# A decode step of cached attention with a gated branch: PE's program cut from three instruction blocks to two by a six-turn loop, h and q ahead of the transposes, nine wo rows and the gate ahead of the last V, PE fillers

## Chip, cores, metric

One core of one Trainium2 chip. The metric is device microseconds of one execution, from repeated runs; the spans in the traces are 1.5 to 2.8 us shorter than the times of the same executions. Profiles are of one execution. PE is TensorE (matmuls), DVE is VectorE, ACT is ScalarE, POOL is GpSimd, and SP is SyncE, which issues the loads. A *filler* is a matmul whose result nobody uses, there to keep PE's clock up; PE is called warm at its full granted clock and cold at half of it. In what follows a "row of wo" is one of the 32 slices of 128x448 into which the output projection is cut; each is one contraction of 128.

## The reference, cut

```python
x = A_x                                   # (2, 1, 448) bf16
xn = _layernorm(x)
# attention over the last W = 2048 of 8192 cached positions, 16 query heads, 8 kv heads, Dh = 256
q = (xn @ wq).reshape(B, 1, 16, 256).transpose(0, 2, 1, 3)
k = repeat(k_cache[:, :, Sk - W:, :], 2, axis=1)
v = repeat(v_cache[:, :, Sk - W:, :], 2, axis=1)
p = softmax(einsum("bhqd,bhkd->bhqk", q, k) * Dh ** -0.5)
s = einsum("bhqk,bhkd->bhqd", p, v) @ wo   # after putting the heads back in a row
g = silu(relu(xn @ w1) @ w2)               # Dff = 1792
return x + s * g
```

44.1 MB are read: K and V 16.8 MB each, wq and wo 3.7 MB each, w1 and w2 1.6 MB each. There are four *turns* (2 batches by 2 halves of the kv heads), each with 4.2 MB of K and 4.2 MB of V.

## The kernel before

A small layer records operations for each engine with their dependencies and then emits waits. PE's turns are one loop; what belongs to only some turns is under a branch. In a turn DVE transposes four blocks of K (the scores need the head dimension on the partitions), PE makes scores from each, and after the softmax the P·V product of the turn *before* is scaled and folded into `at_z`, the left side of the wo product.

```python
def turn(u):
    for blk in range(NBLK):
        if u: do_T(u, blk)                         # DVE transposes
        if u > 1 and blk in (1, 2): ...            # attention fold of turn u-2, between them
        do_S(u, blk)                               # PE scores
    if u: do_PV(u - 1)
    softmax(u)
    if u: attend_scale(u - 1)
    if u == 1: do_H(); do_F()                      # the gated branch; F over four column tiles
    if u < NU - 1: turn_q(u + 1)
# [cut]
for blk in range(NBLK): do_T(0, blk)
do_q(); turn_q(0)
# ... turns 0 to 3, with loads between them; the last V has a buffer of its own (wq's):
#     deps = [None if u == 0 else st["q_mm"] if u == NU - 1 else st["PV", u - 1]]
turn(3)
idle_loop(5, 2)                                    # ten filler matmuls
do_PV(3, (0, 1)); attend_turn(2); do_PV(3, (2,)); attend_spread(2); do_PV(3, (3,))
attend_scale(3)
m_f = fold_tiles(g_ap, True, True, [v_f, v_sel])   # gate, on 8 partitions x 112
# [cut: exp] 
attend_turn(3); attend_spread(3)
m_t = do_wo(0, TILED)                              # nine rows over four column tiles
# [cut: fold of these, add, reciprocal, product of the gate]
m_o = do_wo(TILED, 2 * NWO)                        # 23 rows x 4 matmuls of 112 columns
```

Loads go out from one queue in this order: part of wq, K0, the rest of wq, K1, V0, w1, w2, K2, V1, K3, V2, V3, wo in seven parts. At the start PE jumps to a block near the end of its program and back, so that the last block of instructions is fetched then ("the visit").

Of the kernel before, what the change touches and what calls it, by code (L numbers as in the profile page):

```python
# [14 lines left out]
class _Op:  # L15
    __slots__ = ("eng", "fn", "deps", "dma", "needed", "value", "sem", "turn", "group", "token", "gives")

    def __init__(self, eng, fn, deps, dma):
        self.eng, self.fn, self.deps, self.dma = eng, fn, deps, dma
        self.needed, self.value, self.sem = dma, 0, None  # L20
        self.turn, self.group, self.token, self.gives = None, None, None, False


class _Prog:
# [4 lines left out]
    def __init__(self, nc, es):  # L29
        self.nc, self.es = nc, es  # L30
        self.lists = {PE: [], DVE: [], ACTE: [], SP: [], POOL: []}
        self.turn, self.group, self.runs = None, None, {}

    def op(self, eng, fn, deps=(), token=None):
        o = _Op(eng, fn, [d for d in deps if d is not None], False)
        if eng == PE:
            o.turn, o.group, o.token = self.turn, self.group, token
        self.lists[eng].append(o)
        return o
# [6 lines left out]
    def run(self, turns):  # L46
# [6 lines left out]
        taken = {DVE: [], SP: []}  # L53
        for o in pe:
            if o.token is not None:
                assert not o.token.gives
                o.token.gives = True
                taken[o.token.eng].append(o.token)
        for e in taken:
            assert taken[e] == [o for o in self.lists[e] if o.gives]  # L60
# [16 lines left out]
        for e, ops in self.lists.items():  # L77
            sem, count = self.es.enter_context(nc.semaphore(f"s_{e}")), 0
            for o in ops:
                if o.gives:  # L80
                    assert o.dma or not o.needed
                    o.sem = give[e]
# [3 lines left out]
                elif o.needed:  # L86
                    count += 1
                    o.sem, o.value = sem, count
# [22 lines left out]
        for eng, name in ((nc.vector, "dve"), (nc.tensor, "pe")):  # L111
            again[name] = eng.alloc_register(f"{name}_again")
            nc.br("dve_all" if name == "dve" else "pe_visit", engines=[eng.engine])
# [15 lines left out]
        body = [o for o in loop if o.turn == turns - 1]  # L129
        body += [o for o in loop if o.group == "ffn"]  # L130
        with nc.body("pe_all", parent=main, valid_engines=[t.engine]):
            top = nc.cur_bb
# [3 lines left out]
            with t.Fori(0, turns) as i:  # L136
                k = 0
                while k < len(body):
                    g = body[k].group
                    end = next((m for m in range(k, len(body)) if body[m].group != g), len(body))  # L140
                    part, runs = body[k:end], self.runs[g]
                    k = end
                    if runs == list(range(turns)):
                        emit(t, part, seen)
                    elif len(runs) == 1:
                        with t.If(i == runs[0]):
                            emit(t, part, seen)
                    else:
                        assert runs == list(range(runs[0], turns))
                        with t.If(i > runs[0] - 1):  # L150
                            emit(t, part, seen)
            nc.br("pe_past", engines=[t.engine])
            nc.switch_bb("pe_visit", parent=main)
            t.nop()
            nc.br("pe_all", engines=[t.engine])
            nc.switch_bb("pe_past", parent=top)
# [5 lines left out]
def bass_recurrent_scan__sliding_block_cached__dense_activation_relu__decode_kernel(  # L162
# [21 lines left out]
    NU = 4  # L184
# [9 lines left out]
    FIRST = 2  # L194
    NCOL = D // 4
    NROW = 4 * B
    GAP = NROW + 3
    es = contextlib.ExitStack()
    with es:
# [31 lines left out]
        q_n = named("q_n", [128, 512], BF)  # L231
        qz = named("qz", [128, 4 * 64], BF)
        h_n = named("h_n", [128, FC // 4], BF)
        h_t = named("h_t", [128, FC // 4], BF)
        h_z = named("h_z", [128, 14 * GAP], BF)
        x_c = named("x_c", [NROW, NCOL], BF)
        ea = named("ea", [NROW, NCOL], F32)
        g_sb = named("g_sb", [NROW, NCOL], F32)
        tmp = named("tmp", [NROW, NCOL], F32)
# [8 lines left out]
        q_t = named("q_t", [128, 512], F32)  # L248
        ssum = named("ssum", [128, 1], F32)
# [15 lines left out]
        obk_last = psum("obk_last", [128, 512], F32)  # L265
# [13 lines left out]
        d_xc = pr.dma(ACTE, x_c[:, :], A_x[:, 0, :].rearrange("b (i n) -> (b i) n", i=4))  # L279

# [13 lines left out]
        def load_v(u, cuts=(0, NT)):  # L294
            deps = [None if u == 0 else st["q_mm"] if u == NU - 1 else st["PV", u - 1]]
            d_v[u] = []
            for lo, hi in zip(cuts, cuts[1:]):
                d_v[u].append((hi, pr.dma(SP, vbuf[u // (NU - 1)][:, lo * DH:hi * DH],
                                          kv_src(u, A_v_cache)[:, :, lo * DH:hi * DH], deps)))

        d_wq = [pr.dma(SP, wq_sb[:, 0:FIRST * HC], wq_src[:, 0:FIRST * HC])]
        load_k(0)
        d_wq.append(pr.dma(SP, wq_sb[:, FIRST * HC:SLOTS * HC], wq_src[:, FIRST * HC:SLOTS * HC]))
        load_k(1)
        load_v(0)
        st["w1"] = pr.dma(SP, w1_sb[:, 0:W2_AT], w1_src)
        st["w2"] = pr.dma(SP, w2_sb[:, W2_AT:W2_AT + 14 * D].rearrange("p (hf f) -> p hf f", hf=2), w2_src)
# [5 lines left out]
        p_z = [pr.op(POOL, lambda e, t=t: e.memset(t[:, :], 0.0)) for t in (qrep, spread, sel, h_z, at_z)][-1]  # L313

        a_z = [pr.op(ACTE, lambda e, t=t: e.memzero(t[:, :])) for t in (obk, sbk, hbk, fbk, obk_last)][-1]
# [7 lines left out]
        pr.op(ACTE, lambda e: e.activation(tmp[0:B, 0:1], st2[0:B, 0:1], ACT.Exp), [a_sd])  # L323
        for e2 in range(2):
# [39 lines left out]
        for s in range(SLOTS):  # L364
            m_xr = pr.op(PE, mm(mbk_ap(2 * s, 2), xg[0:B, 128 * s + 128:128 * s + 256], ident[0:B, 0:B], s == 0),
                         [v_xn, p_id])
# [56 lines left out]
        def out_bank(u):  # L423
            return obk if u < NU - 1 else obk_last

        def do_PV(u, gs=range(4)):
            bank, src = out_bank(u), vbuf[u // (NU - 1)]
            for g in gs:
                deps, token = [], None
                if u == NU - 1:  # L430
                    deps = [next(d for hi, d in d_v[u] if hi >= 16 * g + 16), st["pt", u]]
                elif g == 0:
                    token = d_v[u][0][1]
                for a in range(2):
                    for i in range(4):
                        t = 16 * g + 4 * i + 2 * a
                        o = pr.op(PE, mm(bank[32 * i:32 * i + 16, :],
                                         pt[:, 8 * t:8 * t + 16], src[:, t * DH:(t + 2) * DH],
                                         g == 0 and a == 0, g == 3 and a == 1, tile_position=(0, 32 * i)), deps, token=token)
                        deps, token = [], None  # L440
            st["PV", u] = o

        def attend_scale(u):
            st["osb", u] = pr.op(DVE, lambda e: e.tensor_scalar(  # L444
                out=o_sb[:, :], in0=view(out_bank(u), 0, [[1, 512]]), scalar1=rs[:, u:u + 1], scalar2=None, op0=ALU.mult),
                [st["PV", u], st["rs", u], st.get(("oT", u - 1))])

        def attend_turn(u):
            deps = [st["osb", u]] if u > 1 else []
            for dhi in range(2):  # L450
                for tp in range(2):
                    o = pr.op(PE, mm(mbk_ap(136 + 8 * dhi, 8), o_sb[:, 256 * tp + 128 * dhi:256 * tp + 128 * dhi + 128],
                                     fold[:, 8 * tp:8 * tp + 8], tp == 0, tp == 1), deps)
                    deps = []
# [6 lines left out]
        def attend_spread(u):  # L461
# [3 lines left out]
                                      [at] if u > 1 else [], token=None if u > 1 else at)  # L465
# [3 lines left out]
        def do_q():  # L469
            deps = d_wq + [v_xr, a_z]  # L470
# [6 lines left out]
            st["q_mm"] = o  # L477
# [5 lines left out]
        def do_H():  # L483
            deps = [st["w1"]]
            for s in range(SLOTS):
                for i in range(4):
                    lo = s * FC + i * (FC // 4)
                    o = pr.op(PE, mm(hbk[32 * i:32 * i + 4, 0:FC // 4], xr[:, 4 * s:4 * s + 4], w1_sb[:, lo:lo + FC // 4],
                                     s == 0, s == SLOTS - 1, tile_position=(0, 32 * i)), deps)
                    deps = []  # L490
            v = pr.op(DVE, lambda e: e.tensor_scalar(
                out=h_n[:, :], in0=hbk[:, 0:FC // 4], scalar1=0.0, scalar2=None, op0=ALU.max), [o])
            v = pr.op(DVE, lambda e: e.transpose(h_t[:, :], view(h_n, 0, [[1, 7], [7, 32]])), [v])
            st["h"] = pr.op(DVE, lambda e: e.tensor_copy(  # L494
                view(h_z, 3, [[GAP, 7], [7 * GAP, 2], [4, 2]]), view(h_t, 0, [[32, 7], [2, 2], [1, 2]])), [v, p_z])
# [13 lines left out]
        def do_F():  # L509
            deps = [st["w2"], st["h"]]  # L510
            for f in range(14):
                st["F"] = tiled(fbk, h_z, f, w2_sb, W2_AT + f * D, 4, 10, deps)
                deps = []

        def idle_work(n, deps=()):
            for _ in range(n):
                pr.op(PE, mm(wbk[:, :], ident[:, :], q_n[:, :], True, True), deps)
                deps = ()

        def idle_loop(n, m):  # L520
            def fn(e):
                with e.Fori(0, n):
                    for _ in range(m):
                        o = mm(wbk[:, :], ident[:, :], q_n[:, :], True, True)(e)
                return o
            pr.op(PE, fn)

        def turn(u):
            pr.turn, pr.group = u, "all"
            for blk in range(NBLK):  # L530
                if u:
                    do_T(u, blk)
                if u > 1 and blk in (1, 2):
                    pr.group = "turn" if blk == 1 else "spread"
                    (attend_turn if blk == 1 else attend_spread)(u - 2)
                    pr.group = "all"
# [109 lines left out]
```

## Time and profile before

| | before |
|---|---|
| time, median | 113.06 us (4 runs; 113.56 when the prediction was made, of 3) |
| span of the profile | 109.8 us |
| DMA queue busy | 95.0% of the span |
| PE, DVE busy | 55%, 57% |
| last row of wo landed | 107.4 us |
| end of the last wo matmul | 108.0 us |

How to read the profile's lines: in a line of the timeline the first two numbers are the start and the length in us; then engine, source line, operation, what it writes and reads, and in square brackets how long the engine idled before it and for whom. In a line of the windows the columns are the stretch, its length, busy time of PE, PEld (weight loads), DVE, ACT and POOL with their counts, granted PE clock, DMA share and GB/s. The lines of before are in the prediction.

Each load lands on 16 DMA engines, and the records of the trace tell when each of the 16 was done. Worked out from them for the kernel before, first and last engine in us: K0 14.97 to 16.59, K1 30.80 to 32.42, K2 57.86 to 59.49, last part of wo 105.86 to 107.39. The last engine is 1.5 us or more behind the first in every load. Up to K2 it is alone (in K0 the other 15 are done by 15.33).

### The profile page before, as it was taken

The numbers are of one execution on the slowest core, as the hardware profiler recorded it, in microseconds if no ns is written. First come the engines' busy times: TensorE is split into PE (matmuls) and PEld (weight loads), VectorE is DVE, ScalarE is ACT, GpSimd is POOL, SyncE is SP. The second block draws the span as 40 slices with busy tenths as digits, with TensorE's granted clock in tenths as the row PEclk, the third lists the DMA queues.
The fourth block names the chain that finished last, engine by engine and source line by source line (L and its number), as shares of the span: only waits on it lengthen the run. The fifth ranks groups of instructions, "written<-read, shape, count | busy, mean of one in ns | idle before, by whom it ended". The sixth has DMA issues, their size and how long they took to land. (4 is left out here: it accounts for less than half of the span.)

```text
span 109.8 us, 1368 instructions
## 1 busy us (share of the span) xinstructions
PE 60.4 (55%) x558; PEld 19.5 (18%) x558; DVE 63.0 (57%) x96; ACT 10.2 (9%) x19; POOL 3.1 (3%) x11
## 2 busy tenths in 40 slices
PE   0001000076599330899755597853039785898993
PEld 0000000020111020000241010112001011534792
DVE  0249109995400459993468999266299926624601
ACT  4990000000000110000200000020000002000000
POOL 7400000000000000000000000000000000000000
PEclk9999999999999995579996569997555899999999
DMA  3998989998899889998899999999999999899950
GB/s 60 502 388 382 549 371 395 439 537 382 382 453 501 382 367 416 411 548 382 382 501 394 406 406 465 441 406 406 465 441 406 444 430 430 361 419 410 402 207 7
DMA packets 3046, 44.15 MB, mean 402 GB/s; under 512 B 354, under 2 KB 612, under 8 KB 1508
## 3 DMA queue, kind: packets, MB, share of 16 engines
q1 hardware_dynamic: 3008, 44.11, 95.0%
q8 instruction: 2, 0.03, 0.1%
q10 hardware_dynamic: 36, 0.01, 0.1%
HBM read 44.11 MB, written 0.00 MB: 402 GB/s over the span
## 5 line engine op out<-in xcount | busy, mean ns | idle before, releaser
L379 DVE STREAM_TRANSPOSE kt<-kbuf 128x2048 f32<-128x2048 f32 x16 | 35.9, 2286 | 7.8 <-DMA kbuf<-in_A_k_cache_dram 7.8
L361 PE MATMUL sbk<-kt,qz 128*8 128x512 bf16 x128 | 31.1, 1073 | 13.6 <-PEq L102 13.5
L401 DVE TENSOR_REDUCE rm<-sbk 128x1 f32<-128x512 f32 x4 | 2.8, 692 | 14.6 <-PE sbk L361 14.6
L361 PE MATMUL obk<-vbuf,xr 128*4 128x512 bf16 x28 | 3.2, 626 | 13.9 <-DMA vbuf<-in_A_wq_dram 13.9
L407 ACT ACTIVATE et<-sbk,bias 128x512 bf16<-128x512 f32 x4 | 2.7, 687 | 81.1 <-DVE bias L405 81.1
L361 PEld LDWEIGHTS sbk<-kt,qz 128*8 128x8 bf16 x128 | 2.6, 87 | 28.9 <-issue 28.7
L361 PE MATMUL pbk<-et,spread 128*128 128x32 bf16 x64 | 2.6, 193 | 7.2 <-PEq L102 7.2
L361 PE MATMUL obk<-vbuf,pt 128*16 128x512 bf16 x96 | 5.8, 381 | 0.0
L361 PE MATMUL mbk<-ident,xg 2*128 2x2 bf16 x7 | 0.3, 163 | 8.5 <-DVE xg L325 8.5
L361 PE MATMUL wbk<-q_n,ident 128*128 128x512 bf16 x15 | 4.1, 395 | 1.4 <-DVE qz L396 1.4
L361 PE MATMUL hbk<-kbuf,at_z 128*8 128x112 bf16 x92 | 4.8, 213 | 0.0
L409 DVE STREAM_TRANSPOSE et<-et 128x512 bf16<-128x512 bf16 x4 | 2.8, 712 | 3.4 <-ACT et L407 3.4
L417 DVE TENSOR_TENSOR pt<-pbk,hmask 128x512 bf16<-128x512 f32 x4 | 2.8, 692 | 3.3 <-PE pbk L361 3.3
L361 PEld LDWEIGHTS hbk<-kbuf,at_z 128*8 128x8 bf16 x92 | 4.6, 87 | 0.1
L361 PEld LDWEIGHTS pbk<-et,spread 128*128 128x128 bf16 x64 | 2.2, 99 | 10.5 <-issue 10.5
L361 PEld LDWEIGHTS obk<-vbuf,pt 128*16 128x16 bf16 x96 | 2.5, 94 | 6.8 <-issue 4.7
L361 PEld LDWEIGHTS obk<-vbuf,xr 128*4 128x4 bf16 x28 | 0.8, 114 | 15.4 <-issue 15.4
L611 DVE TENSOR_TENSOR tmp<-hbk,g_sb 8x112 f32<-8x112 f32 x1 | 0.3, 262 | 4.4 <-PE hbk L361 4.4
L361 PE MATMUL fbk<-wf,h_z 128*2 128x448 bf16 x14 | 1.7, 567 | 1.7 <-DVE h_z L494 1.7
L456 DVE TENSOR_TENSOR at_exp<-mbk,qmask 128x128 bf16<-128x128 f32 x4 | 1.2, 292 | 2.5 <-PE mbk L361 2.5
L361 PE MATMUL obk_last<-vbuf,pt 128*16 128x512 bf16 x32 | 2.3, 380 | 0.0
L444 DVE TENSOR_SCALAR o_sb<-obk,rs 128x512 bf16<-128x512 f32 x3 | 2.2, 731 | 0.0
(80 smaller groups left out, 43.9 us busy)
## 6 DMA issues: line engine op xcount, KB each, us to landing
kbuf<-in_A_k_cache_dram SPq DMA_DIRECT2D x4, 4096.0 KB, 23.4
vbuf<-in_A_v_cache_dram SPq DMA_DIRECT2D x3, 4096.0 KB, 15.8
wf<-in_B_w_dram SPq DMA_DIRECT2D x2, 1568.0 KB, 42.4
vbuf<-in_A_v_cache_dram SPq DMA_DIRECT2D x1, 3072.0 KB, 22.5
vbuf<-in_A_wq_dram SPq DMA_DIRECT2D x1, 2560.0 KB, 20.9
vbuf<-in_A_wq_dram SPq DMA_DIRECT2D x1, 1024.0 KB, 6.1
vbuf<-in_A_v_cache_dram SPq DMA_DIRECT2D x1, 1024.0 KB, 24.4
kbuf<-in_A_wo_dram SPq DMA_DIRECT2D x1, 1008.0 KB, 26.2
```

The lines of the kernel that those rows point to most:

```text
L361: return lambda e: e.matmul(out_ap, lhsT=lhsT, rhs=rhs, start=start, stop=stop, skip_group_check=True, **kw)
L379: st["kt", u, blk] = pr.op(DVE, lambda e: e.transpose(view(dst, 0, [[1, 32 * NT]]), view(src, 32 * blk, [[DH // 2, NT], [1, 32]])), [d_k[u ...
L401: v = pr.op(DVE, lambda e: e.tensor_reduce(out=rm[:, :], in_=sbk[:, :], axis=AX.X, op=ALU.max), [st["S", u, NBLK - 1]])
L407: a = st["exp", u] = pr.op(ACTE, lambda e: e.activation(e_sb, sbk[:, :], ACT.Exp, bias=bias[:, 0:1], accum_out=ssum[:, 0:1]), [v, st.get(( ...
L409: token = pr.op(DVE, lambda e: e.transpose(e_t, e_sb), [a, st.get(("Pt", u - 1))])
L417: st["pt", u] = pr.op(DVE, lambda e: e.tensor_tensor(out=view(pt, 0, [[8, NT], [2, 4], [1, 2]]), in0=view(pbk, 0, [[2, NT], [0, 4], [1, 2] ...
L444: st["osb", u] = pr.op(DVE, lambda e: e.tensor_scalar(out=o_sb[:, :], in0=view(out_bank(u), 0, [[1, 512]]), scalar1=rs[:, u:u + 1], scalar ...
L456: st["at", u] = pr.op(DVE, lambda e: e.tensor_tensor(out=view(at_exp, 0, [[16, 8], [8, 2], [1, 8]]), in0=view(mbk, 136, [[1, 8], [8, 2], [ ...
L611: v_t = pr.op(DVE, lambda e: e.tensor_tensor(out=tmp[:, :], in0=hbk[0:NROW, 0:NCOL], in1=g_sb[:, :], op=ALU.mult), [m_o, v_g])
```

## The change

Its intent: PE's program in two 16 KB blocks instead of three, so that no visit is needed. For that the last P·V moves into the loop (six turns instead of four, groups of operations switched by branches), V3 shares the buffer of V0 to V2, h is made by a loop with register addresses, and wo takes two wide matmuls a row instead of four narrow ones. h and q are ready before the first transposes; the gate and nine wo rows are done while V3 is on its way, with sixteen fillers to keep PE's clock up. The core of the diff, cut:

```diff
-        for blk in range(NBLK):
-            do_T(0, blk)
         do_q()
         turn_q(0)
-        idle_work(1, [st["q"]])
+        m_h = do_H()
+        for blk in range(NBLK):
+            do_T(0, blk)
+            if blk == 1:
+                relu(m_h)
+        pr.op(PE, None, [st["q"]])
@@ turn
+            if u > 1:
+                pr.group = "turn"
+                attend_turn(u - 2)
+                attend_spread(u - 2)
+            if u == NU:
+                pr.group = "ffn"
+                do_F()
+                early_wo()
+                idle_loop(FILL, 2)
@@ loads
-            deps = [None if u == 0 else st["q_mm"] if u == NU - 1 else st["PV", u - 1]]
+            deps = [st["PV", u - 1] if u else None]
         load_v(2)
-        load_v(3, (0, 48, 64))
+        load_w2()
+        turn(3)
         for n in WO_PARTS:
             d_wo[j0] = pr.dma(SP, wo_sb[...], wo_src[...], [st["S", 2, NBLK - 1]])
+            if j0 == 0:
+                load_v(3)
@@ do_F: F untiled, gate on 2 partitions x 448
-                st["F"] = tiled(fbk, h_z, f, w2_sb, W2_AT + f * D, 4, 10, deps)
+                st["F"] = pr.op(PE, mm(view(fbk, 0, [[1, D]], n=B), ..., f == 0, f == 13), deps)
+            v_rc = pr.op(DVE, lambda e: e.reciprocal(tmp[0:B, :], ea[0:B, :]), [v_d])
@@ early_wo
+            deps = [pr.op(DVE, lambda e: e.tensor_copy(sums[:, :], view(tbk, 0, [[1, D]])), [m_t]), v_sel]
+            for t in range(2):
+                pr.op(PE, mm(view(hbk, 0, [[1, NCOL]], n=B, p0=32 * t), view(sel, 3, [[4, 2]]), sums[...],
+                             True, tile_position=(0, 32 * t)), deps)
@@ run
-            nc.br("dve_all" if name == "dve" else "pe_visit", engines=[eng.engine])
+            nc.br(f"{name}_all", engines=[eng.engine])
```

## The prediction

> **What bounds the kernel now.** I read the page's head first, then the DMA queues, the chain of waits, the timeline of the first 35 us and of the last 15 us, and the windows around the end.
>
> The page: engine busy shares, the busy tenths in 40 slices, the DMA queues.
>
> ```profile
> PE 60.4 (55%) x558; PEld 19.5 (18%) x558; DVE 63.0 (57%) x96; ACT 10.2 (9%) x19; POOL 3.1 (3%) x11
> DMA  3998989998899889998899999999999999899950
> q1 hardware_dynamic: 3008, 44.11, 95.0%
> q8 instruction: 2, 0.03, 0.1%
> ```
>
> No compute engine is above 57%, while the one DMA queue is busy 95% of the span and only its first and its last slices are thin. 44.11 MB have to come in; the kernel before is a stream of loads. Two instruction fetches lie in the span, about 16 KB each (0.03 MB by 2).
>
> Windows of equal kind around the end of the stream (PE, PEld, DVE, ACT, POOL busy, clock, DMA share, GB/s):
>
> ```profile
> 105.00:105.50 0.50, 0.50 (x14) 0.50 (x12) 0.00 (x0) 0.00 (x0) 0.00 (x0) 1.00 0.97 357
> 105.50:107.50 2.00, 2.00 (x43) 1.89 (x41) 0.00 (x0) 0.00 (x0) 0.00 (x0) 1.00 0.18 67
> 107.50:109.80 2.30, 0.49 (x8) 0.32 (x8) 0.52 (x2) 0.00 (x0) 0.00 (x0) 1.00 0.03 8
> ```
>
> Most of the 16 DMA engines are done by 105.5, a straggler runs to about 107. PE loads weights almost without a gap until 107.3, then starts its last eight matmuls, which end at 108.0. So the chain of waits, which ends in PE's `hbk` work, is level with the last landing: the stream and the tail end together.
>
> The timeline of the tail (start, us, engine, line, operation):
>
> ```profile
> 90.57 0.69 DVE L401 TENSOR_REDUCE rm<-sbk 128x1 f32<-128x512 f32 x1 [2.17 <-PE sbk L361]
> 94.52 2.32 PE L361 MATMUL wbk<-q_n,ident 128*128 128x512 bf16 x10
> 94.98 0.73 DVE L444 TENSOR_SCALAR o_sb<-obk,rs 128x512 bf16<-128x512 f32 x1
> 96.77 1.04 PE L361 MATMUL obk_last<-vbuf,pt 128*16 128x512 bf16 x16
> 99.24 0.75 DVE L444 TENSOR_SCALAR o_sb<-obk_last,rs 128x512 bf16<-128x512 f32 x1 [0.32 <-PE obk_last L361]
> 100.95 0.23 DVE L466 CAST at_z<-mbk 128x16 bf16<-128x16 f32 x1 [0.28 <-PE mbk L361]
> 102.53 0.84 DVE L607 RECIPROCAL tmp<-ea 8x112 f32<-8x112 f32 x1
> 103.20 4.79 PE L361 MATMUL hbk<-kbuf,at_z 128*8 128x112 bf16 x92
> 108.03 0.26 DVE L611 TENSOR_TENSOR tmp<-hbk,g_sb 8x112 f32<-8x112 f32 x1 [4.37 <-PE hbk L361]
> ```
>
> The reader is to see the distance from the last max (`rm`, 90.57) to the end, 19.3 us, and that the reciprocal of 8x112 takes 0.84 us where the add on the same tile took 0.20.
>
> **What the Trainium skill says.** "TensorE: Matmul & The Clock Gate", Part 1: the array runs at half rate after about 3.4 us of idleness and is warm again after about as long a busy window, 426.7 or 215.7 ns for 512 columns. The trace agrees: ten fillers in 2.32 us are 232 ns each, and q's 28 matmuls after a long idle time, four at a time, took 3.16 us, 0.45 us per four. "Runtime: NRT & Kernel Launch", Instruction fetch mechanics: instructions come in blocks of 16 KiB (256 of them) over DMA. PE's program before has 322 matmuls of two instructions each and 38 others, about 682, three blocks; the new one has 196 and 59, about 451, two blocks. The trace has the fetches, but not whose. "VectorE: DVE Perf Modes", First, the fixed hardware budget: the reciprocal is an iterative divide with a repeat count of 8. The trace agrees in kind: 0.84 us for 112 columns, 0.16 for the single column of `rs`, so 6.1 ns for each further column. "SBUF — State Buffer", Door 1: each step to another 16-byte line costs the matmul's read. The score matmuls, which read every eighth bf16, need 1.97 us per eight; the P·V ones, contiguous, 1.92 us per 32.
>
> **The change, part by part.**
>
> *Start.* wq comes whole, then w1, then K0. From the first landings (K0 at 16.6 after 5.24 MB, q's wq at 22.7 after 7.86 MB) the stream does 0.43 MB/us. New landings if the straggler stays: wq 13.0, w1 16.8, K0 26.5, K1 36.2, V0 45.9, K2 55.6. The 1.2 us straggler I put down to the 16 KB fetch into a busy queue at the start: the third PE block, which the added visit at the start pulled in. Two blocks take it away, so 1.2 us earlier: K0 25.3, K2 54.4. q (3.2 us of matmuls, 0.7, 0.7 and 0.5 us of DVE) is done by 19. h uses 49 weight loads with a 14-byte step; at the score matmuls' rate (1.97/8, 0.25 us) about 12 us, 17 to 29, just before its relu stands in DVE's queue (29.8).
>
> *Turns.* Four transposes are 8.9 us, relu 0.2, from their end to `rm` 2.2, from `rm` to the next transposes 4.8 (turn 0) and, with the attention fold now ahead of them (0.29 + 0.19 and two PE trips on top of 0.73 and 0.49), 6.4. So `rm` falls at 36.6, then 36.6+4.8+8.9+2.2 = 52.5, then 70.0, then 87.5; before it was at 90.57.
>
> *Stream.* V1 may go out only when P·V of turn 0 is done, 3.9 us after the transposes (50.42 to 54.29 before), 50.3 + 3.9: 54.2, just when K2 has landed. A first packet is seen about 1 us after its issue (issue 0.74, packets from 1.7), so the queue runs dry for 1 to 1.5 us. V3, now in the buffer of V0 to V2, waits for P·V of turn 2 at 89.3; w2 and nine wo rows fill the queue until 91.5, so little is lost there. V3 lands near 101.3, the last wo row near 107.7: the stream ends where it ended before (107.4).
>
> *Tail.* This is where I see the cost. Nothing may start in P·V of V3 until, in program order, PE has done F, nine wo rows, the fold and 16 fillers, and the fold waits for a DVE copy that stands behind the gate. From `rm` of turn 3:
> - softmax to scaled o: 5.1 (95.71-90.57); fold, spread and at_z 1.2 more: 6.3.
> - F: 14 matmuls of 448 columns one after another, 0.19 us warm and 0.37 cold (the filler's and q's rates): 2.7 to 5.3, taken 4: 10.4.
> - exp of 2x448: 0.65 (0.69 for 512 columns). Add 0.5. Reciprocal 0.16 + 448 x 6.1 ns: 2.9, against 0.84 when it lay on 8 partitions. Two products of 224 columns 0.75 (0.26 for 112). The copy into sums 0.61. With hand-overs 5.7: 16.1.
> - fold 1.0: 17.1. Sixteen fillers of 512: 3.7 warm, 6.9 cold; PE has stood idle 4 us, so taken 5.5: 22.6.
> - P·V of V3: 32 matmuls 2.0: 24.6. Scale to at_z, as before (99.24 to 101.18), 2.0: 26.6.
> - 46 wo matmuls at 52 ns (4.79/92) 2.4: 29.0. Two DVE steps of 224 columns 0.8 instead of 0.55, then 1.3 to the end: 31.1.
>
> All warm it is 27.6, all cold 34. The end of the span is then 87.5 plus 31.1, 118.6; all warm 115.1. Against 109.8 that is 5 to 9 us more. What the change saves is true but hidden: half the wo matmuls (92 to 46 after the nine), a shorter PE program, one DVE step for h instead of three.
>
> **The rivals.**
> 1. The tail is hidden: if gate and fillers end before V3 lands (101.3), the span is the stream's: 107.7, four matmuls 0.4, 0.8 and 1.3, 110.2: about +0.4, and the time 113 to 114.5. For it: this is plainly what the order was built for, and the copy into sums comes at 103.6 only by my estimate of F and of the reciprocal. Against: even with F and fillers warm P·V starts at 87.5 + 19.1, 106.6, 5 us after V3.
> 2. Without the straggler and with no dry queue the stream ends at 106.2, and 108.7 in all, 1% faster. For it: the fetch of 0.03 MB and the idle DMA engines from 105.5 to 107.4. Against: V1's issue at 54.2.
> 3. h is slower than 12 us: every microsecond past 29.8 moves all turns, the dry queue and the tail, one for one. The 14-byte step speaks for it; that a weight load overlaps the matmuls, against.
> 4. PE's loop with branches crosses blocks and fetches in the middle of a full queue. The count, 451 of 512, speaks against it.
>
> **Range and chances.** The time of before is 113.56, 3.7 above the span of its profile, which I carry over. The tail case gives 118.8 (warm) to 124, 122.3 in the middle; I put 85% on it. The hidden-tail case near 114 has the rest. Weighted (0.85 x 122.3 + 0.15 x 114) that is 121; since the errors I know of in the sum are its cold assumptions, I go a little lower: 120.5 us, 115.5 to 124.5. Chances: faster 0.04, same 0.12, slower 0.84.
>
> **What would show it.** Right: P·V of the last V starts well after V3 has landed and straight behind the fillers; the DMA share falls to nothing several us before PE ends; the chain of waits runs through the gate's DVE lines (a reciprocal near 3 us) and `wbk`, not through a wo landing; only one instruction packet, at the end. The queue is thin for about 1 us near 55. `rm` of the last turn near 87.5. Wrong: P·V waits for V3's DMA after the fillers, the wo matmuls are paced by landings and the span is near 110. Or h's matmuls pass 31 us, which would make the number too low for another reason.

## The result and the profile after

The changed kernel takes 122.97 us (median of 4, 122.22 to 123.24) against 113.06 us of the same rounds; the ratio is 1.087, 95% interval 1.077 to 1.097. Ratios here are the mean time of one kernel's fast runs over that of the other's fast runs of the same rounds, so not quite the ratio of the medians. Executions over 1.5% slower than the fastest of the same kernel are left out of the means. The span grew from 109.8 to 120.3 us.

The page of the changed kernel, the lines that answer to those of before:

```profile
PE 70.6 (59%) x522; PEld 23.8 (20%) x522; DVE 64.8 (54%) x94; ACT 10.9 (9%) x20; POOL 3.5 (3%) x13
DMA  5998999999999999966898989898999999990000
q1 hardware_dynamic: 2964, 44.11, 87.3%
q8 instruction: 1, 0.02, 0.0%
```

The same bytes, but the queue's share is down from 95% to 87%: the last four slices, 12 us, are all but empty, and there is a dent at slices 18 and 19. One instruction fetch instead of two.

Windows around the dent and over the tail:

```profile
53.00:54.00 1.00, 1.00 (x26) 0.40 (x16) 0.85 (x4) 0.01 (x1) 0.00 (x0) 1.00 0.08 33
54.00:55.00 1.00, 0.30 (x8) 0.00 (x0) 0.20 (x1) 0.77 (x2) 0.00 (x0) 1.00 0.00 0
93.80:104.90 11.10, 6.31 (x25) 2.02 (x27) 4.93 (x6) 0.53 (x1) 0.00 (x0) 0.65 0.98 416
104.90:111.50 6.60, 6.60 (x24) 2.14 (x28) 0.00 (x0) 0.00 (x0) 0.00 (x0) 0.60 0.54 205
111.50:118.10 6.60, 4.65 (x84) 2.91 (x83) 1.27 (x3) 0.00 (x0) 0.00 (x0) 1.00 0.00 0
```

A window's DMA share is uneven by the way packets are counted (some windows show over 1), but from 54.32 to 55.67 the trace has not one packet. From 111.5 on nothing is left to load, and 6.6 us of PE and DVE work in turns (PE busy for 4.65) and two last DVE steps are still to come.

The timeline of the tail:

```profile
87.61 0.69 DVE L407 TENSOR_REDUCE rm<-sbk 128x1 f32<-128x512 f32 x1 [2.17 <-PE sbk L360]
89.33 1.20 SPq L45 DMA_DIRECT2D vbuf<-in_A_v_cache_dram  x2
...
94.02 4.64 PE L360 MATMUL fbk<-wf,h_z 128*2 128x448 bf16 x12 [0.23 <-issue]
...
99.44 0.53 ACT L511 ACTIVATE q_t<-fbk 2x448 f32<-2x448 f32 x1 [9.69 <-PE fbk L360]
...
100.42 2.94 DVE L514 RECIPROCAL tmp<-q_t 2x448 f32<-2x448 f32 x1
103.40 0.77 DVE L516 TENSOR_TENSOR g_sb<-fbk,tmp 2x224 f32<-2x224 f32 x2
104.20 0.62 DVE L540 COPY sums<-tbk 128x448 f32<-128x448 f32 x1
...
104.88 0.91 PE L360 MATMUL hbk<-sums,sel 128*2 128x224 f32 x4 [4.57 <-DVE sums L540]
...
105.73 5.81 PE L360 MATMUL wbk<-spread,ident 128*128 128x512 bf16 x16
...
111.47 1.90 PE L360 MATMUL obk<-vbuf,pt 128*16 128x512 bf16 x32
113.43 0.75 DVE L442 TENSOR_SCALAR o_sb<-obk,rs 128x512 bf16<-128x512 f32 x1 [8.60 <-PE obk L360]
...
115.70 2.37 PE L360 MATMUL hbk<-kbuf,at_z 128*2 128x224 bf16 x46 [0.49 <-DVE at_z L464]
```

V3 had landed at 103.50 and the last wo row at 109.96 (landings from the trace's records), yet P·V of V3 begins at 111.47, right behind the last filler. The reader should follow the chain by hand here: the printed chain of waits reaches back only to 115.0 (`mbk` and `at_z`). PE idles 4.57 us for the copy into `sums`, and the copy stands behind the reciprocal of 2.94 us. Before it, F runs at half clock: 12 matmuls in 4.64 us; the granted clock was 0.65 in that window.

What of the prediction's steps the trace gives, us:

| step | predicted | measured |
|---|---|---|
| K0 landed | 25.3 | 25.60 |
| `rm` of turns 0, 1, 2, 3 | 36.6, 52.5, 70.0, 87.5 | 36.78, 52.62, 69.97, 87.61 |
| V1 issued; stretch without packets | 54.2; 1 to 1.5 | 54.35; 1.35 |
| V3 issued; landed | 89.3; 101.3 | 89.33; 103.50 |
| last wo row landed | 107.7 | 109.96 |
| `rm` to end of at_z | 6.3 | 6.44 |
| F | 4 (2.7 to 5.3) | 5.36 to 99.41 |
| exp to the end of the copy | 5.7 | 5.4 |
| fold, fillers | 1.0, 5.5 | 0.91, 5.8 |
| P·V, scale to at_z | 2.0, 2.0 | 1.9, 2.05 |
| wo, two DVE steps, rest | 2.4, 0.8, 1.3 | 2.4, 0.8, 1.4 |
| end of span | 118.6 | 120.3 |

### The profile page after: what moved, and what is told of

Same layout as the page of the kernel before. It is cut to its first block, busy times and chain, and to the rows that moved or that the text cites. A ratio compares the mean times of both kernels' runs of the same rounds, so it can differ in the third digit from the quotient of the medians.

```text
span 120.3 us, 1436 instructions
## 1 busy us (share of the span) xinstructions
PE 70.6 (59%) x522; PEld 23.8 (20%) x522; DVE 64.8 (54%) x94; ACT 10.9 (9%) x20; POOL 3.5 (3%) x13
## 5 line engine op out<-in xcount | busy, mean ns | idle before, releaser
L360 PE MATMUL hbk<-xr,wf 128*128 x49 | 6.9, 208 | 2.5 <-issue 2.5
L360 PE MATMUL mbk<-ident,xg 2*128 2x2 bf16 x7 | 1.2, 178 | 11.9 <-DVE par L329 9.0
L360 PE MATMUL obk<-vbuf,pt 128*16 128x512 bf16 x128 | 7.7, 381 | 0.0
L360 PEld LDWEIGHTS hbk<-xr,wf 128*128 x49 | 6.2, 131 | 3.3 <-issue 3.0
L360 PE MATMUL wbk<-spread,ident 128*128 128x512 bf16 x16 | 5.8, 544 | 0.0
L360 PE MATMUL fbk<-wf,h_z 128*2 128x448 bf16 x14 | 5.4, 574 | 0.2 <-issue 0.2
L360 PEld LDWEIGHTS obk<-vbuf,pt 128*16 128x16 bf16 x128 | 3.2, 93 | 7.9 <-issue 5.1
L360 PE MATMUL mbk<-fold,o_sb 128*128 128x8 bf16 x16 | 1.0, 166 | 5.2 <-PEq L105 5.2
L360 PE MATMUL hbk<-sums,sel 128*2 128x224 f32 x4 | 0.9, 555 | 4.6 <-DVE sums L540 4.6
L360 PEld LDWEIGHTS mbk<-ident,xg 2*128 x7 | 0.7, 99 | 12.3 <-issue 12.3
## 6 DMA issues: line engine op xcount, KB each, us to landing
kbuf<-in_A_wo_dram SPq DMA_DIRECT2D x1, 1008.0 KB, 19.4
```

Source lines behind the costliest of these rows:

```text
L360: return lambda e: e.matmul(out_ap, lhsT=lhsT, rhs=rhs, start=start, stop=stop, skip_group_check=True, **kw)
```

## The experiments

Eight kernels ran, in two groups of four; each group shares its runs of the kernel before on one chip, whose median was 111.35 us in the first and 112.48 us in the second. So ratios, not times, are to be compared between groups. All results were correct. Theory 1 is the prediction's: a serial PE and DVE path at the end. Theory 2: the stream, with its dry stretch and its late V3, sets the end. Both would make the kernel slower, so they had to be told apart.

**e1: no fillers.**

```diff
-                idle_loop(FILL, 2)
```

> The changed kernel without its sixteen fillers. Theory 1 (the time is lost in a serial tail: gate on DVE, then the copy into sums, the fold, the fillers and only then P.V of the last V): the fillers stand on that path with 5.8 us, so P.V starts at about 105.7 instead of 111.5; but the array is then cold, P.V takes 3.5 instead of 1.9 us and the 46 wo matmuls up to 4.3 instead of 2.4, so the end comes 2 to 4 us earlier: span 116.5 to 118.5, time about 119 to 121. Theory 2 (the stream with its dry queue and the late V3 sets the end): fillers fill a wait, taking them away changes nothing or makes the end later by the cold clock: 120 or more.

Measured: ratio 1.056 (1.047 to 1.065), median 118.89 us. The profile fell in one of its two slow runs (119.70; the fast ones are 117.73 and 118.09), so the lines show the order of events; the sizes are those of that slow run:

```profile
104.79 0.92 PE L360 MATMUL hbk<-sums,sel 128*2 128x224 f32 x4 [4.91 <-DVE sums L540]
105.33 3.79 PE L360 MATMUL obk<-vbuf,pt 128*16 128x512 bf16 x32
...
111.45 3.36 PE L360 MATMUL hbk<-kbuf,at_z 128*2 128x224 bf16 x46 [0.49 <-DVE at_z L464]
```

P·V starts 6.1 us earlier, but in this slow run takes 3.79 instead of 1.90 us and wo 3.36 instead of 2.37: of 5.8 us of fillers 2.9 come back as a cold array. The spans of the two fast runs are 115.9 and 116.3, against 119.7 to 120.6 of the changed kernel: about 4 us less. Theory 1 said 2 to 4, a span of 116.5 to 118.5 and a time of 119 to 121, so its direction holds and its size was a little low; theory 2 (120 or more) is missed clearly. Here the fillers on the path cost more than they save.

**e2: one DVE instruction moved.**

```diff
 [F, then on DVE:]
-   gate: add, reciprocal, two products
    copy into sums          (the fold on PE waits for it)
+   gate: add, reciprocal, two products
```

> The changed kernel with one DVE instruction moved: the copy into sums ahead of the gate's four instead of behind them. Nothing is added or removed. Theory 1: the fold starts about 4 us earlier (near 101 instead of 104.9), PE has not stood idle, the fillers run warm (3.7 instead of 5.8), P.V starts at 105.7 to 107: span 114 to 116, time about 117 to 118.5. Theory 2: same as the changed kernel, 122.9.

Measured: ratio 1.052 (1.045 to 1.059), 117.29 us, span 114.8, both inside the ranges of theory 1.

```profile
99.61 0.62 DVE L542 COPY sums<-tbk 128x448 f32<-128x448 f32 x1 [5.75 <-PE tbk L360]
...
100.55 2.94 DVE L516 RECIPROCAL tmp<-q_t 2x448 f32<-2x448 f32 x1
...
104.32 1.90 PE L360 MATMUL obk<-vbuf,pt 128*16 128x512 bf16 x32
...
108.61 4.03 PE L360 MATMUL hbk<-kbuf,at_z 128*2 128x224 bf16 x46 [0.55 <-DVE at_z L464]
```

Not one instruction was taken away, and P·V starts 7.2 us earlier (1.4 us before the range expected): the fold no longer waits for the gate (it starts at 100.28 instead of 104.88, 4.6 us), and the fillers, with PE busy just before, run warm in 3.4 instead of 5.8 us. The gain at the end is 5.5 us; the wo matmuls gave 1.7 us back to the clock, which fell to half at 108.9. Theory 2 cannot give this: no load was touched.

**e3: the fold behind the last P·V, no fillers.**

```diff
-            deps = [pr.op(DVE, lambda e: e.tensor_copy(sums[:, :], ...), [m_t]), v_sel]
+            st["sums"] = pr.op(DVE, lambda e: e.tensor_copy(sums[:, :], ...), [m_t])
+        def late_fold():
+            deps = [st["sums"], v_sel]
-                idle_loop(FILL, 2)
         turn(NU + 1)
+        late_fold()
```

> The changed kernel without fillers and with the fold of the nine wo rows behind the last P.V instead of ahead of it, so P.V waits for V3 alone. Theory 1: P.V starts when the end of V3 lands (103.5 in the changed kernel), cold; at_z by 109, the wo matmuls by 111.5 to 113.5: span 113.5 to 115.5, time 116 to 118. Theory 2: the last wo row lands at 110, so the span can't be under 112.3; it would stay above 118.

Measured: ratio 1.022 (1.014 to 1.031), 114.46 us. That is 1.5 us under the low end expected. The profile, of a slow run (115.39 us), has a span of 113.7; the fast runs have 111.5 to 113.2, under the expected 113.5 too, and two of them under the 112.3 that theory 2 allowed. P·V of the first three quarters began with V3's first part, at 99.96, which I had not counted, so at_z was ready at 106.15 and not at 109; the wo matmuls then ran cold in 4.51 us and ended at 111.47.

**e4: copy first, four fillers.**

```diff
-    FILL = 8
+    FILL = 2
 [and the order of e2]
```

> The copy into sums ahead of the gate, and four fillers instead of sixteen, which end before V3 lands. Theory 1: the tail is hidden as the change meant it; P.V starts at V3's landing (103.5), wo ends with the last landing (110): span 112.3 to 113.5, time 115 to 116. What is then left over before (109.8) is the stream's own loss: the dry queue near 55 us and V3's late landing, some 3 us. Theory 2: at 120 as the changed kernel.

Measured: ratio 1.030 (1.023 to 1.038), 114.97 us, span 112.2, both at the low end of theory 1's ranges or a hair under. The intervals of e3 and e4 overlap.

```profile
101.57 1.47 PE L360 MATMUL obk<-vbuf,pt 128*16 128x512 bf16 x24
103.20 0.61 PE L360 MATMUL obk<-vbuf,pt 128*16 128x512 bf16 x8 [0.16 <-PEq L105]
...
108.44 0.93 PE L360 MATMUL hbk<-kbuf,at_z 128*2 128x224 bf16 x10 [0.30 <-DMA kbuf<-in_A_wo_dram]
109.59 0.36 PE L360 MATMUL hbk<-kbuf,at_z 128*2 128x224 bf16 x4 [0.21 <-DMA kbuf<-in_A_wo_dram]
```

Now, and in none of the kernels of e1 to e3, the releaser of the last wo matmuls is a load (109.54). This is the prediction's first rival, the hidden tail, made real: its span was put at 110.2 and is 112.2, because the last row lands at 109.5 and not at 107.7. The reorder and the filler count are worth 8.1 of the 10.5 us of span between these profiles (by the ratios, 1.087 to 1.030, about two thirds of the loss); 2.4 us remain, and they are the stream's: its last row lands 2.15 us later than in the kernel before.

**e5: a third block and the visit, put into the changed kernel.**

```diff
-            nc.br(f"{name}_all", engines=[eng.engine])
+            nc.br("dve_all" if name == "dve" else "pe_visit", engines=[eng.engine])
+            nc.switch_bb("pe_pad", parent=main)      # 90 matmuls that never run
+            for _ in range(PAD):
+                self.pad(t)
+            nc.switch_bb("pe_visit", parent=main)    # then back to pe_all
```

> The changed kernel with 90 matmuls that never run behind its end, so that its PE program has three blocks of 16 KB, and with the kernel before's visit to the last block at the start. Theory 1 (the straggler of the kernel before is the fetch of that block into a busy queue): one fetch near 2 us in the trace, one DMA engine 1.2 us behind the others in every landing from then on (spread 1.5 instead of 0.8 us), K0 at 26.5 instead of 25.6, all turns and so the end about 1 us later: time about 123.9. Theory 2 (the straggler has another cause, such as the first DMA's shape): no change to landings or time, 122.9.

Measured: 122.94 us, ratio 1.100 (1.089 to 1.111); e6 of the same rounds has 1.100 too, and the changed kernel itself, 1.087, comes from another group, so the time tells nothing here. The landings do. First and last of the 16 DMA engines, in us, worked out of the trace's records:

```
                     K0              K1              K2              V1
changed kernel   24.74-25.60     34.45-35.31     53.90-54.73     66.39-66.75
e5               24.65-26.48     34.37-36.19     53.82-55.62     67.27-67.61
```

There is a 16 KB fetch at 1.82 us that takes 1.88 us (and one at 8.7 us), and the last DMA engine is a microsecond further behind, in K0, K1 and K2 alike. A second engine is 0.7 us behind the other 14 (25.48, 26.20 and 26.48 for the last three in K0): two fetches and two late engines, where the kernel before has one early fetch and one late engine. `rm` of the last turn is at 88.39 instead of 87.61. So the first part of the expectation holds, but "in every landing from then on" was wrong: after the dry stretch the spread is 0.34 us. An engine that is behind catches up when all the others have to wait for the next load. The microsecond itself does not fall into the dry stretch. V1 may go out only after P·V of turn 0, which hangs on K0, so the whole stretch moves: it lasts 1.38 us as before (1.35), V1 lands 0.86 us later and `rm` comes 0.78 us later. What of this reaches the end can't be read here: the span is 0.7 us longer (121.0), but in this execution F and the fillers took 1.6 us less and the wo matmuls 1.5 us more (3.90), by the granted clock.

**e6: w2 in two halves, the first ahead of V1.**

```diff
         load_k(2)
+        load_w2(0)
@@
         load_v(2)
-        load_w2()
+        load_w2(1)
```

> The changed kernel with w2 in two halves, the first queued ahead of V1. Theory 1 (the tail's PE and DVE path sets the end): the dry stretch near 55 us (1.35 us without any packet) goes away, K3 and V3 land as before or a little earlier, but the end does not move: span 119.5 to 120.8, time 122 to 123.5. Theory 2 (the stream sets the end): 2 us faster, near 120.8.

Measured: 123.34 us, inside the range, ratio 1.100 (1.090 to 1.110); the span of 121.1 is 0.3 above its range. The windows at 53 to 55 us:

```profile
53.00:54.00 1.00, 1.00 (x24) 0.55 (x16) 0.82 (x4) 0.05 (x1) 0.00 (x0) 1.00 0.52 215
54.00:55.00 1.00, 0.28 (x8) 0.00 (x0) 0.24 (x1) 0.73 (x2) 0.00 (x0) 1.00 1.05 439
```

The dry stretch is gone, V3 lands at 101.76 instead of 103.50 and the last row at 108.30 instead of 109.96 (about 1 us of this is one slow engine in the profile of the changed kernel; the first of the 16 has V3 0.64 us earlier), and the kernel ends no earlier. Theory 2 falls as the cause of the 10 us. A shorter dry stretch (0.5 us) appears in front of V3.

**e7: the changed kernel mended.**

```diff
 [the order of e2, no fillers, the halves of e6, and:]
-            if j0 == 0:
+            if j0 == WO_PARTS[0]:
                 load_v(3)                 # behind two parts of wo
+            for j in range(TILED, NWO): ...   # rows 9 to 15 ahead of the last P.V
         turn(NU + 1)
+        gate_out()                        # the gate's two products behind the last at_z
```

> The changed kernel mended: copy into sums ahead of the gate, no fillers, the gate's two products behind the last at_z, w2 in halves as above, V3 queued behind two parts of wo instead of one, and rows 9 to 15 of wo done ahead of the last P.V. If both the tail and the dry queue are what the change lost: V3 lands near 102.2, at_z near 105.3, the last wo row near 107: span 109.2 to 110.2, time 111.5 to 112.5, equal to the kernel before within 1%. If something else keeps it slow (PE's loop with its branches, the late K0): above 112.

Measured: 112.60 us as the median of six runs, of which three are slow (112.86 to 113.60). The three fast ones took 111.15 to 112.34, where 111.5 to 112.5 was expected; ratio of fast runs 0.998 (0.986 to 1.010), span 109.8, a fast run.

```profile
102.73 0.61 PE L360 MATMUL obk<-vbuf,pt 128*16 128x512 bf16 x8 [0.43 <-PEq L105]
103.39 0.75 DVE L442 TENSOR_SCALAR o_sb<-obk,rs 128x512 bf16<-128x512 f32 x1 [0.40 <-PE obk L360]
...
105.73 1.82 PE L360 MATMUL hbk<-kbuf,at_z 128*2 128x224 bf16 x32 [0.55 <-DVE at_z L464]
107.59 0.38 DVE L628 TENSOR_TENSOR tmp<-hbk,g_sb 34x224 f32<-34x224 f32 x1 [1.53 <-PE hbk L360]
```

V3 lands at 102.60, the last row at 107.15, the wo matmuls end at 107.55: stream and tail are level again, as in the kernel before. What the change lost is accounted for, within the 1% of the interval, by the order of its tail and by its queue; its loop, its branches and the late K0 cost nothing that is seen at the end. It is no faster than before either. A likely reason, which no run tests, is that V3 may not start until the P·V of turn 2 is done (89.5), while before it sat in its own buffer and landed at 98.5.

**b0: the kernel before without the visit.**

```diff
-            nc.br("dve_all" if name == "dve" else "pe_visit", engines=[eng.engine])
+            nc.br(f"{name}_all", engines=[eng.engine])
-            nc.br("pe_past", engines=[t.engine])
-            nc.switch_bb("pe_visit", parent=main)
-            t.nop()
-            nc.br("pe_all", engines=[t.engine])
-            nc.switch_bb("pe_past", parent=top)
```

> The kernel before without the visit to its third PE block at the start, nothing else changed. If the fetch at 2 us makes the straggler, the landings come 1 us earlier until the block is fetched later, on its own account; then either that later fetch costs less (span 108.8 to 109.5, up to 1% faster) or PE waits for it in a full queue or fetches blocks again in each turn of its loop (span above 110.5, slower). If the straggler has another cause: same as before.

Measured: 111.57 us, ratio 0.997 (0.990 to 1.004), span 110.1: between the two branches of the expectation, so the same. The page and the records:

```profile
q8 instruction: 1, 0.02, 0.1%
```

```
                     K0              K1              V0              last wo
before           14.97-16.59     30.80-32.42     40.52-42.14     105.86-107.39
b0               14.77-15.41     30.60-31.24     40.32-42.41     105.57-107.63
```

With the visit gone the 16 DMA engines land within 0.64 us of each other, until PE's third block is fetched at 33.1 us. That fetch takes 1.06 us, and from the next load on one engine is 2.1 us behind and stays so to the end. Moving the fetch gained nothing; what a program without it gains at the end was not isolated. With e5, where adding the fetch brought the late engine, this settles what makes the straggler.

## Why the prediction was right

*The bound.* "The stream and the tail end together" is a reading of the trace of before (last landing 107.4, last wo matmul 108.0). e7, where both again end together, comes out within 1% of before, which fits; no run changed only one of the two in the kernel before.

*The tail.* This was named as the cost, and its terms came out as the table shows. One sign failed in form: the printed chain of waits doesn't run through the gate's lines, and the waits in the timeline had to be followed instead. The one clearly mis-sized term is F, 5.36 us against 4: its matmuls ran at the cold rate of 0.37 us throughout, the end of the stated range. With it the sum is 32.7 instead of 31.1 us from `rm` to the end. That the other terms fit so closely is in part luck, because they hang on when the clock is granted: e5 and e6 have the same tail, and there F took 4.5 and 5.4 us, the fillers 5.1 and 5.5, the wo matmuls 3.9 and 3.5 instead of 2.4, and the sums 32.6 and 33.6. The 2.4 us of the wo matmuls were also carried over from matmuls half as wide, without a reason. e2 shows that the fold's wait for the gate is the hinge, e1 that the fillers are on the path, e6 that the stream is not.

*The number.* 120.5 was given, 122.97 measured; the sum itself said 122.3. That it came so near is luck: its span was 1.7 us short (118.6 against 120.3), and the 3.7 us added for time over span were 1.3 us too many (2.4 in the profiled run), because the median of three timed runs of before was set against the span of the profiled one, which was faster than any of them (111.31 us with a span of 109.8, 1.5 apart). From 122.3 the weight of 15% on the hidden tail took 1.3 us, and 0.5 more came off since the cold assumptions looked too dear; F showed the opposite. The hidden tail needs an order of DVE and a number of fillers that the change does not have; e4 has them. The weight was caution, not working. Some sums are also off: all warm, the listed terms give 28.0 and not 27.6 us (P·V after 19.4, not 19.1), and all cold, 34 us lead to 125.2 us and not to 124, outside the stated range. The rates for F, 0.19 and 0.37 us, are not those of the fillers and of q, which give 0.20 and 0.39; they are the 215.7 and 426.7 ns that it quotes, scaled to 448 columns.

*The stream.* The straggler's cause and the dry stretch in front of V1 were right. The loss was mis-sized: 1 to 1.5 us of silence were predicted and 1.35 came, but V1 landed 12.0 us after K2 (54.73 to 66.75), where loads in an unbroken queue follow at 9.7. So the loss is 2.3 us. After the dry stretch the spread is down from 0.83 to 0.36 us, so its other use, letting the last engine catch up, was small here. V3 then lost another microsecond to one slow engine (99.59 to 100.99 for its first part, spread 1.4 us); in the other runs that spread is 0.3 to 1.1, and no run explains it. This had no effect on the end of the changed kernel.

*The rivals.* The first (hidden tail) is refuted for the change and realised by e4. The second (stream 1.2 us shorter) is right about the straggler: K0 landed earlier without it (25.60 against 26.48 in e5). But it also needed a queue that never runs dry, and the queue did. In e7, where the trace shows no dry stretch, the last row still landed at 107.15 and not at 106.2. The third, slow h, did not happen: h ran from 17.8 to 27.2, 9.4 and not 12 us, a weight load of 14-byte step costing 131 ns instead of the estimated 250. The fourth, fetches in the middle, did not happen: the only fetch is at 119.3, at the end.

## What to carry to other kernels

When work is moved "into a wait", read for each engine what stands ahead of the end of that wait in program order: here a 0.62 us copy queued behind a 2.94 us reciprocal held PE for 4.6 us, and the fillers that were to bridge a wait became the path. Narrow layouts that are harmless off the path (a gate on 2 partitions, untiled matmuls) must be summed up before they are put in front of a dependent chain. In a kernel that is one stream of loads, sum the queue's landings against every issue that waits for compute: one buffer shared by two loads can empty the queue.

## What the Trainium skill lacked or had wrong

- "Runtime: NRT & Kernel Launch" (Instruction fetch mechanics) calls the price of crossing a 16 KB block mostly hidden. On PE it was hidden (in b0 PE is busy throughout 33 to 34 us), but not for the data, of which the page says nothing: one such fetch put one of the 16 DMA engines 1.4 us further behind (spread 0.64 to 2.09 us in b0), and it stayed behind until the end of the stream.
- "DMA: Bandwidth & Descriptors" (Latency and other measured facts) gives about 0.6 us to the first byte. When the queue had run dry, the first packet came 1.3 us after the issue began (54.35 to 55.67; 0.8 us after the 0.54 us of the issue ended), and the load landed 2.3 us later than in an unbroken queue.
- "SBUF — State Buffer" (Door 1) has a penalty for each step to a new 16-byte line, but no size for it. The score matmuls, whose moving side steps so, take four times as long as those of P·V (no run isolates the step); a weight load with a 14-byte step took only 131 ns, against 99 for a packed one of 128 columns.
- No page that names the reciprocal on DVE has a price per column for it: 0.84 us for 112 columns, 2.94 for 448, 6.25 ns for each further column, the first on 8 partitions, the second on 2.
